# An attention and gated-FFN kernel on one Trainium2 core: two products go from VectorE to GpSimd, and the head gets ten more matmuls

## The chip, the core and the metric

The kernel runs on one core of a Trainium2 chip. Five engines work side by side, each through its own list of instructions in order: TensorE (PE in the profile, its weight loads PEld), VectorE (DVE), ScalarE (ACT), GpSimd (POOL) and SyncE (SP), which here issues nearly all of the transfers. They meet through semaphores. The metric is the device time of one execution in microseconds.

## The reference, cut to what matters

Inputs are float32: x of 1 x 2048 x 512, wqkv 512 x 1536, wo 512 x 512, w1 and w3 512 x 1792, w2 1792 x 512.

```
xn  = layernorm(x)                              # over the 512
q,k,v = split(xn @ wqkv)                        # 32 heads of 16
p   = softmax(q k^T / 4)                        # full, 2048 x 2048 for each head
s   = (p v for all heads, side by side) @ wo
h   = silu(xn @ w1) * (xn @ w3)
g   = silu(h @ w2)
out = x + s * g
```

In the reference the layer-normalised xn feeds both the attention and the gated network.

## The kernel before, in words

**Stages.** A head of some 160 us normalises and transposes x, splits each operand of the projections into a high and a low part (a product is then three matmuls), and computes q, k and v. Then comes the long steady part, up to about 1640 us, and a tail that multiplies by wo and adds x.

**The steady part** is 32 *phases*: 16 pairs of heads times two halves of the queries. Three kinds of products share PE. For the exponentials, L625 makes a 128 x 512 tile of scores in a PSUM bank and ACT turns it into exponentials (L628). For the row maxima of the next phase, L389 makes such a tile and DVE reduces it (L391). For the gated network ("gate"), L855 adds up halves of products in a third kind of bank. All three use only half of PE's rows, so two of them run side by side. Between them, groups of L638 multiply the exponentials by the values into one fixed bank `pv`, whose row 17 of each 32 collects the sums. Seven banks are shared by the three kinds; a bank comes back when ACT or DVE has read it.

**What sets the order.** PE's order is a string of some 8,700 letters, `ORDER_OF_ISSUE`: s and S for scores, m and M for maxima, f and F for gate halves, v for values. While the program is written out, a small model of the engines (`Model`) keeps estimated times; steps of the other engines are put into their lists when the model says that their input is ready. `soon(engine, ready, ...)` books such a step of the gate, and `settle()` writes it out when its time has come. `mod.work(engine, start, cost)` books an engine's estimated time.

**End of a phase.** `take_out` (L641 to L665) is a chain of steps, some microseconds of model time apart: ACT copies `pv` to `ot` (L644); SP spreads the sums over 128 partitions (L650); DVE takes reciprocals (L652); SP writes them out (L654) and reads them back, broadcast, into the one tile `rb` (L657); 16 us of model time later the product `ot * rb` follows (L659, DVE), then POOL rounds it to a high part `oh` (L662) and takes the low part `ol` (L663); SP stores both (L674). The last three phases go another way, so 29 pass here.

**The gate** (`gate`, L706) runs over four blocks of 512 tokens, each in two halves of the 1792. POOL does its products (L725, L726, L741 to L743) and splits the streamed weights w1, w3, w2 (L321, L322; the weights come through L307, four raw tiles in flight, splits up to five units ahead). At the end of each block four row tiles close (`summed`, L756): DVE adds the second half's sum to `part` (L765, `add`), ACT takes a tanh (L771, `bend`), one product makes silu from it (L775, `times`), and SP stores the tile (L776). A silu is written as y * (1 + tanh) with the factors of a half left for later.

**The head.** `busy(n)` (L447) runs n transposes of the identity into `pv`, whose content nobody reads: 12 at the start and 6 more behind the first tile's transposes (L479). Behind them stand the first token tile's value products (L506).

Of the kernel before, what the change touches and what calls it, by code (L numbers as in the profile page):

```python
# [12 lines left out]
ALU = mybir.AluOpType  # L13
# [127 lines left out]
def raw(ap):  # L141
    return ap.bitcast(F32)
# [3 lines left out]
def kernel(ctx: ExitStack, tc: tile.TileContext, x, wqkv, wo, w1, w3, w2, out):  # L146
    nc = tc.nc
# [40 lines left out]
    rb = const.tile([P, 512], F32, name="rb")  # L188
# [20 lines left out]
    def xt_pair(pool):  # L209

        return [pool.tile([P, KC, 512], F32R, tag=f"xt{v}", name=f"xt{v}", bufs=1) for v in "hl"]
# [84 lines left out]
    mod = Model()  # L296
# [120 lines left out]
    with tc.tile_pool(name="pro", bufs=1) as pro, tc.tile_pool(name="pros", bufs=1) as pros:  # L417
# [29 lines left out]
        def busy(n):  # L447
            for _ in range(n):
                nc.tensor.transpose(pv[:, :P], ident, ident)

        busy(12)
        xts = {}

        def spread(t):
# [186 lines left out]
    def take_out(p, half):  # L641

        ot = work.tile([P, 512], F32, tag="ot", name="ot", bufs=2)
        nc.scalar.copy(ot, pv)  # L644
        yield
        sums = work.tile([P, 16], F32, tag="sums", name="sums", bufs=2)
        rec = work.tile([P, 16], F32, tag="rec", name="rec", bufs=2)
        rd = dram.tile([4, 512], F32, name=f"rd{p * 2 + half}")
        for j in range(4):
            nc.sync.dma_start(sums[32 * j:32 * j + 32, :], ot[32 * j + DH:32 * j + VW, :])  # L650
        yield
        nc.vector.reciprocal(rec, sums)  # L652
        yield
        nc.sync.dma_start(rd.rearrange("j (a b) -> (j a) b", b=16), rec)  # L654
        yield
        for j in range(4):
            nc.sync.dma_start(rb[32 * j:32 * j + DH, :], rd[j:j + 1, :].to_broadcast([DH, 512]))  # L657
        yield
        nc.vector.tensor_mul(ot, ot, rb)  # L659
        oh = work.tile([P, 512], F32R, tag="oh", name="oh", bufs=1)  # L660
        ol = work.tile([P, 512], F32R, tag="ol", name="ol", bufs=1)
        nc.gpsimd.tensor_scalar(oh, ot, 1.0, 1.0, op0=ALU.mult, op1=ALU.mult)  # L662
        nc.gpsimd.tensor_sub(ol, ot, raw(oh))  # L663
        yield
        store_rows(p, half, oh, ol)  # L665

    def store_rows(p, half, oh, ol):
        for qb in range(2):
            for h in range(2):
                j, r = 32 * (qb * 2 + h), (p % 4) * 32 + h * DH  # L670
                for s, v in enumerate((oh, ol)):
                    b = half * 2 + qb
                    dst = raw(o_d[p // 4][s][b]) if p < NP - 1 else raw(ov[b][s][p // 4])
                    nc.sync.dma_start(dst[r:r + DH, :], raw(v)[j:j + DH, :])  # L674
# [5 lines left out]
    def soon(engine, ready, bank, what):  # L680

        owed.append((ready, engine, bank, what))
        owed.sort(key=lambda e: e[0])
# [8 lines left out]
    def flush(bank):  # L692

        while any(e[2] <= bank for e in owed):
            e = next(e for e in owed if e[2] <= bank)
            owed.remove(e)
            e[3](e[0])

    def three(lhs, rhs):

        return [(lhs[1], rhs[0]), (lhs[0], rhs[1]), (lhs[0], rhs[0])]
# [4 lines left out]
    def gate():  # L706

        xt = xts[TB - 1]
        number = 0
        for n, b in enumerate(ORDER):  # L710
            part = {}
            for hf in range(HF):
                hs = []
                u = [None]

                def gated(ps, i, u=u):
                    th = ffn.tile([P, 512], F32, tag="th", name="th", bufs=2)
                    nc.scalar.activation(th, ps, AF.Tanh, scale=0.5)
                    mod.work("act", lanes.begins + mod.LATENCY, 0.6)
                    g = u[0] = ffn.tile([P, 512], F32, tag="u", name="g", bufs=2)  # L720
                    nc.scalar.copy(g, ps)
                    free_at[lanes.at_bank[i]] = mod.work("act", 0.0)

                    def times(ready):
                        nc.gpsimd.tensor_scalar(th, th, 1.0, 1.0, op0=ALU.add, op1=ALU.mult)  # L725
                        nc.gpsimd.tensor_mul(g, th, g)  # L726
                        mod.work("pool", ready, 1.9)

                    soon("pool", free_at[lanes.at_bank[i]], i, times)

                def upped(ps, i, f, hs=hs, u=u):
                    if not hs:
                        hs.extend(ffn.tile([P, FH, 512], F32R, tag=f"hs{v}", name="hs", bufs=1) for v in range(2))
                    flush(i - 1)
                    g = u[0]
                    h2 = ffn.tile([P, 512], F32, tag="th", name="h2", bufs=2)
                    nc.scalar.copy(h2, ps)  # L737
                    free_at[lanes.at_bank[i]] = mod.work("act", lanes.begins + mod.LATENCY)

                    def times(ready):  # L740
                        nc.gpsimd.tensor_mul(h2, g, h2)  # L741
                        nc.gpsimd.tensor_scalar(hs[0][:, f, :], h2, 1.0, 1.0, op0=ALU.mult, op1=ALU.mult)
                        nc.gpsimd.tensor_sub(hs[1][:, f, :], h2, raw(hs[0][:, f, :]))  # L743
                        made[i] = mod.work("pool", ready, 3.2)

                    soon("pool", free_at[lanes.at_bank[i]], i, times)

                first = number
                for f in range(FH):
                    for up in range(2):  # L750
                        i, w = wts.next()
                        mms = [m for k in range(KC) for m in three([v[:, k, :] for v in w], [v[:, k, :] for v in xt])]
                        yield lambda j, mms=mms: mms[j], 3 * KC, [i], (lambda ps, i, f=f: upped(ps, i, f)) if up else gated, None
                        number += 1

                def summed(ps, i, t, hf=hf, part=part, b=b):  # L756
                    if hf == 0:
                        part[t] = ffn.tile([P, 512], F32, tag=f"part{t}", name="part", bufs=1)
                        nc.scalar.copy(part[t], ps)
                        free_at[lanes.at_bank[i]] = released[i] = mod.work("act", lanes.begins + mod.LATENCY)  # L760
                        return
                    y = part[t]

                    def add(ready):
                        nc.vector.tensor_add(y, y, ps)  # L765
                        free_at[lanes.at_bank[i]] = released[i] = mod.work("dve", ready, 0.7)
                        soon("act", released[i], i, bend)

                    def bend(ready):
                        th = ffn.tile([P, 512], F32, tag="u", name="th2", bufs=2)  # L770
                        nc.scalar.activation(th, y, AF.Tanh, scale=0.25)  # L771
                        soon("dve", mod.work("act", ready, 0.6), i, lambda ready: times(ready, th))

                    def times(ready, th):
                        nc.vector.scalar_tensor_tensor(y, th, 1.0, y, op0=ALU.add, op1=ALU.mult)  # L775
                        soon("sync", mod.work("dve", ready, 0.7) + 0.3, i, lambda ready: nc.sync.dma_start(  # L776
                            g_d[b][t * P:(t + 1) * P, :], y))

                    soon("dve", lanes.begins + mod.LATENCY, i, add)

                ws = []
                for t in range(4):

                    def down(j, t=t, first=first, hs=hs, ws=ws):
                        f = j // 3
                        flush(first + 2 * f + 1)
                        if f == len(ws):
                            ws.append(wts.next())
                        w = [v.rearrange("p a b -> p (a b)") for v in ws[f][1]]
                        return three([v[:, f, t * P:(t + 1) * P] for v in hs], w)[j % 3]  # L790

                    if t > 1 and hf == 1 and n + 1 < TB:
                        if t == 2:
                            xt = xt_pair(keep)
                        nc.sync.dma_start(raw(xt[t - 2]).rearrange("p k t -> p (k t)"), raw(xt_d[ORDER[n + 1]][t - 2]))
                    yield down, 3 * FH, [i for i, _ in ws] if t == 3 else [], (
                        lambda ps, i, t=t: summed(ps, i, t)), first
                    number += 1
# [299 lines left out]
    ready = {0: 0.5}  # L1098
# [185 lines left out]
    ot, oh, ol = pt_tile(F32), pt_tile(F32R), pt_tile(F32R)  # L1284
# [20 lines left out]
    for t in range(4):  # L1305
        i, ps = take("o")
# [30 lines left out]
```

## Time and profile before

| | |
|---|---|
| median of three runs | 1761.44 us (1761.28 to 1761.94) |
| profiled execution | 1762.41 us |
| its span, first to last instruction | 1760.3 us |
| PE busy | 99% of the span |
| DVE busy | 84% |
| ACT busy | 71% |
| POOL busy | 40% |
| granted TensorE clock, as the profile gives it | 1.000 |

Rows of instruction groups read: line, engine, operation, tiles out<-in, shapes, count, then total busy us and mean ns of one, then the engine's idle time just before them and what ended it. Rows of waits read: who <- for whom, us in total, times, longest. Rows of a timeline begin with the start in us and the duration; in brackets stands the idle time before it. Rows of stretches read: from:to, length, busy us and count of instructions of each engine named, then granted clock, share of the DMA engines, GB/s. PE's ends are modelled, so its busy time covers short holes between matmuls.

### The profile page before, as it was taken

Reading aid. Unit: us, or ns where it says so; the run is one execution under the profiler, and the core shown is the slowest. Engines: PE = TensorE matmul, PEld = TensorE weight load, DVE = VectorE, ACT = ScalarE, POOL = GpSimd, SP = SyncE. Lnnn points to the kernel's source line nnn. Section 1 sums busy time; section 2 is a strip of 40 time slices with the busy share of each in tenths; the row PEclk is TensorE's granted clock in tenths of the full one; section 3 lists DMA queues with packets and bytes.
Section 4 is the critical chain, followed back from the end, with each engine's and each line's share of the span. In section 5 each row is a group of like instructions: output and inputs, shape, how many; then the busy total and the mean of one; then the engine's idle time right before and its main releaser. Section 6 shows DMA issues by size and latency. Waiting matters only on the chain.

```text
span 1760.3 us, 35527 instructions
## 1 busy us (share of the span) xinstructions
PE 1747.2 (99%) x13178; PEld 1028.4 (58%) x13178; DVE 1480.8 (84%) x2452; ACT 1253.5 (71%) x2376; POOL 699.5 (40%) x730
## 2 busy tenths in 40 slices
PE   9999999999999999999999999999999999999998
PEld 7877655555555555555555555565555565556455
DVE  6567998889888998898898898898988897899725
ACT  4223778778768787778778777777777867868871
POOL 3102743346425460545236442555155615551101
PEclk9999999999999999999999999999999999999999
DMA  8656213132323221231433131132322221330542
GB/s 276 243 200 206 59 40 70 47 70 59 74 81 84 59 58 47 61 81 47 92 97 68 51 77 32 50 68 74 100 79 62 74 44 53 100 90 28 186 147 96
DMA packets 146797, 155.36 MB, mean 88 GB/s; under 512 B 42304, under 2 KB 100672, under 8 KB 143648
## 3 DMA queue, kind: packets, MB, share of 16 engines
q1 hardware_dynamic: 145760, 151.52, 31.2%
q8 instruction: 104, 1.70, 0.4%
q10 hardware_dynamic: 864, 1.57, 0.2%
q14 instruction: 69, 0.57, 0.1%
HBM read 107.97 MB, written 44.02 MB: 86 GB/s over the span
## 4 chain that ended last, share of the span: by engine, by line
PE 90%; issue 4%; DVE 3%; DMA 1%; ACT 1%; SPq 1%; POOL 0%; DVEq 0%; ACTq 0%; POOLq 0%
PE pv L638 26%; PE f L855 25%; PE e L625 17%; PE m L389 13%; PE m L506 3%; DVE mp L391 2%; PE e L195 2%; PE e L199 2%; PE e L197 2%; DVE ot L659 1%; ACT pt L628 1%; PE m L479 0%; PE m L403 0%; DMA inh<-in_A_x_dram 0%; SPq L892 0%
## 5 line engine op out<-in xcount | busy, mean ns | idle before, releaser
L391 DVE TENSOR_REDUCE mp<-m 128x1 f32<-128x512 f32 x2048 | 1299.1, 684 | 162.4 <-PE m L389 93.0
L628 ACT ACTIVATE pt<-e 128x512 f32<-128x512 f32 x2048 | 1092.8, 604 | 318.7 <-PE m L389 133.0
L625 PE MATMUL e<-qs,ks 64*128 64x512 f32 x2048 | 717.3, 415 | 2.8 <-DVE mp L391 2.6
L389 PE MATMUL m<-ks,qs 62*128 62x512 f32 x2048 | 694.3, 412 | 1.6 <-DVE mp L391 1.1
L638 PE MATMUL pv<-pt,vt 128*17 128x512 f32 x4096 | 515.0, 597 | 0.0
L625 PEld LDWEIGHTS e<-qs,ks 64*128 64x128 f32 x2048 | 340.0, 184 | 273.0 <-ACT pt L628 92.2
L389 PEld LDWEIGHTS m<-ks,qs 62*128 62x128 f32 x2048 | 336.8, 184 | 129.2 <-ACT pt L628 42.5
L638 PEld LDWEIGHTS pv<-pt,vt 128*17 128x17 f32 x4096 | 81.3, 96 | 201.7 <-issue 193.0
L855 PE MATMUL f<-xth,wl 64*128 64x512 f32 x488 | 171.9, 397 | 0.0
L855 PE MATMUL f<-xtl,wh 64*128 64x512 f32 x488 | 171.7, 392 | 0.0
L855 PE MATMUL f<-xth,wh 64*128 64x512 f32 x488 | 169.4, 393 | 0.0
L741 POOL TENSOR_TENSOR h<-g,h 128x512 f32<-128x512 f32 x56 | 72.0, 1285 | 213.3 <-ACT h L737 213.2
L662 POOL TENSOR_SCALAR oh<-ot 128x512 fp32r<-128x512 f32 x29 | 18.3, 630 | 337.6 <-DVE ot L659 304.8
L855 PE MATMUL f<-wh,hs 64*128 64x512 f32 x496 | 149.8, 396 | 0.0
L855 PE MATMUL f<-xth,xel 64*128 64x512 f32 x408 | 147.9, 396 | 0.0
L855 PE MATMUL f<-xth,xeh 64*128 64x512 f32 x408 | 144.9, 392 | 0.0
L855 PE MATMUL f<-xtl,xeh 64*128 64x512 f32 x408 | 144.3, 392 | 0.0
L322 POOL TENSOR_TENSOR wl<-wr,wh 128x512 fp32r<-128x512 f32 x92 | 118.8, 1291 | 7.7
L855 PE MATMUL f<-xeh,hs 64*128 64x512 f32 x400 | 121.2, 393 | 0.0
L322 POOL TENSOR_TENSOR xel<-wr,xeh 128x512 fp32r<-128x512 f32 x76 | 97.9, 1289 | 6.3
L855 PEld LDWEIGHTS f<-xtl,wh 64*128 64x128 f32 x488 | 85.7, 185 | 6.8
L855 PEld LDWEIGHTS f<-xth,wh 64*128 64x128 f32 x488 | 84.6, 185 | 6.4
(178 smaller groups left out, 1994.0 us busy)
## 6 DMA issues: line engine op xcount, KB each, us to landing
wr<-in_B_w_dram SPq DMA_DIRECT2D x168, 256.0 KB
qs<-qk SPq DMA_DIRECT2D x186, 64.0 KB
ks<-qk SPq DMA_DIRECT2D x90, 128.0 KB
qk<-sh SPq DMA_DIRECT2D x32, 256.0 KB
qk<-sl SPq DMA_DIRECT2D x32, 256.0 KB
v<-vrow SPq DMA_DIRECT2D x16, 272.0 KB
xin<-in_A_x_dram SPq DMA_DIRECT2D x16, 256.0 KB
g<-part SPq DMA_DIRECT2D x16, 256.0 KB
```

Source lines behind the costliest of these rows:

```text
L195: nc.tensor.matmul(ps, lhs[1], rhs[0], start=first, stop=False)
L197: nc.tensor.matmul(ps, lhs[0], rhs[1], start=False, stop=False)
L199: nc.tensor.matmul(ps, lhs[0], rhs[0], start=False, stop=last)
L322: nc.gpsimd.tensor_sub(lo, t, raw(hi))
L389: nc.tensor.matmul(ps, qs[p % 2][64 * h:64 * h + KM, q0:q0 + P], ks[p % 2][64 * h:64 * h + KM, c * 512:(c + 1) * 512], start=True, stop=True)
L391: nc.vector.reduce_max(mp[p, half][:, h, qt, c:c + 1], ps, axis=AX.X)
L506: nc.tensor.matmul(ps, lhs, wsp[k][h == 1][:, 2 * D:], start=n == 0, stop=n == len(three) - 1)
L625: nc.tensor.matmul(ps, ks[p % 2][64 * h:64 * h + KR, k * P:(k + 1) * P], qs[p % 2][64 * h:64 * h + KR, q0:q0 + 512], start=True, stop=True)
L628: nc.scalar.activation(pt, ps, AF.Exp, scale=DH ** -0.5)
L638: nc.tensor.matmul(pv[32 * j:32 * j + VW, :], vt[2 * p // GH][:, key, 2 * p % GH + j % 2, :], pt, start=key < 2 if last else k == 0, stop= ...
L741: nc.gpsimd.tensor_mul(h2, g, h2)
L855: nc.tensor.matmul(ps, left[r], right[r], start=starts and lane == 0, stop=ends and lane == 1)
```

## The change

Three edits. The first `busy` has 22 transposes in place of 12. In `take_out`, the product `ot * rb` is POOL's in place of DVE's. In the gate's `times`, DVE's one instruction (th + 1) * y becomes two of POOL's, one that adds 1 to th in place and one that multiplies; the step is booked on POOL with 1.9 us of model time, where it was booked on DVE with 0.7.

```diff
-        busy(12)
+        busy(22)
...
-        nc.vector.tensor_mul(ot, ot, rb)
+        nc.gpsimd.tensor_mul(ot, ot, rb)
         oh = work.tile([P, 512], F32R, tag="oh", name="oh", bufs=1)
         ol = work.tile([P, 512], F32R, tag="ol", name="ol", bufs=1)
         nc.gpsimd.tensor_scalar(oh, ot, 1.0, 1.0, op0=ALU.mult, op1=ALU.mult)
...
-                        soon("dve", mod.work("act", ready, 0.6), i, lambda ready: times(ready, th))
+                        soon("pool", mod.work("act", ready, 0.6), i, lambda ready: times(ready, th))
 
                     def times(ready, th):
-                        nc.vector.scalar_tensor_tensor(y, th, 1.0, y, op0=ALU.add, op1=ALU.mult)
-                        soon("sync", mod.work("dve", ready, 0.7) + 0.3, i, lambda ready: nc.sync.dma_start(
+                        nc.gpsimd.tensor_scalar(th, th, 1.0, 1.0, op0=ALU.add, op1=ALU.mult)
+                        nc.gpsimd.tensor_mul(y, th, y)
+                        soon("sync", mod.work("pool", ready, 1.9) + 0.3, i, lambda ready: nc.sync.dma_start(
                             g_d[b][t * P:(t + 1) * P, :], y))
```

Behind the head PE's list is the same as before, and so is ACT's. In the changed kernel lines from 777 on have a number higher by one. Three places show what moves.

DVE, where the first gate block closes its last two tiles beside the end of a phase (about 517 us of the profile before). `mp` are the maxima, `part` the gate's tile. Before:

```order
L391 TENSOR_REDUCE mp<-m 128x1 x6
L765 TENSOR_TENSOR part<-part,f 128x512
L391 TENSOR_REDUCE mp<-m 128x1
L775 SCALAR_TENSOR_TENSOR part<-th_7144,part 128x512
L659 TENSOR_TENSOR ot<-ot,rb 128x512
L391 TENSOR_REDUCE mp<-m 128x1 x8
L765 TENSOR_TENSOR part<-part,f 128x512
L391 TENSOR_REDUCE mp<-m 128x1
L775 SCALAR_TENSOR_TENSOR part<-th_7309,part 128x512
```

With the change, the same place:

```order
L407 TENSOR_TENSOR ml<-m,mh 16x128
L391 TENSOR_REDUCE mp<-m 128x1 x6
L765 TENSOR_TENSOR part<-part,f 128x512
L391 TENSOR_REDUCE mp<-m 128x1 x9
L765 TENSOR_TENSOR part<-part,f 128x512
L391 TENSOR_REDUCE mp<-m 128x1 x13
```

The two products between the maxima are gone; the sum L765 stays on DVE.

POOL at the same place (`wh`, `wl`, `xeh`, `xel` are weight splits). Before:

```order
L742 TENSOR_SCALAR hs<-h_6446 128x512
L743 TENSOR_TENSOR hs<-h_6446,hs 128x512
L662 TENSOR_SCALAR oh<-ot 128x512
L663 TENSOR_TENSOR ol<-ot,oh 128x512
L321 TENSOR_SCALAR wh_7291<-wr 128x512
L322 TENSOR_TENSOR wl_7292<-wr,wh_7291 128x512
```

With the change, from the block's third tile on:

```order
L775 TENSOR_SCALAR th_7156<-th_7156 128x512
L776 TENSOR_TENSOR part<-th_7156,part 128x512
L659 TENSOR_TENSOR ot<-ot,rb 128x512
L662 TENSOR_SCALAR oh<-ot 128x512
L663 TENSOR_TENSOR ol<-ot,oh 128x512
L321 TENSOR_SCALAR wh_7304<-wr 128x512
L322 TENSOR_TENSOR wl_7305<-wr,wh_7304 128x512
L321 TENSOR_SCALAR xeh<-wr 128x512
L322 TENSOR_TENSOR xel<-wr,xeh 128x512
```

The block's third product (L775, L776) and the phase's product (L659) now stand ahead of the rounding and the splits; the block's fourth product comes behind four splits.

SP, stores and loads at the end of the first gate block. Before:

```order
L650 DMA sums<-ot 32x1x16 x4
L776 DMA g_126<-part 128x512
L795 DMA xth<-xt_66 128x2048
L654 DMA rd_6546<-rec 128x16
L657 DMA rb<-rd_6546 16x512 x4
L776 DMA g_126<-part 128x512
```

With the change:

```order
L650 DMA sums<-ot 32x1x16 x4
L777 DMA g_126<-part 128x512
L796 DMA xth<-xt_66 128x2048
L654 DMA rd_6556<-rec 128x16
L657 DMA rb<-rd_6556 16x512 x4
L777 DMA g_126<-part 128x512
```

Here the order is the same, with each store of g now waiting for POOL; elsewhere a store of g stands a few transfers later than before.

## The prediction

> **What bounds the kernel now.** I read the page first, then the groups of instructions, then the waits of the weight loads, and last the stretches just behind the instructions that the change removes.
>
> ```profile
> span 1760.3 us, 35527 instructions
> PE 1747.2 (99%) x13178; PEld 1028.4 (58%) x13178; DVE 1480.8 (84%) x2452; ACT 1253.5 (71%) x2376; POOL 699.5 (40%) x730
> L391 DVE TENSOR_REDUCE mp<-m 128x1 f32<-128x512 f32 x2048 | 1299.1, 684 | 162.4 <-PE m L389 93.0 <-PE e L625 43.6 <-PE f L855 13.4
> L659 DVE TENSOR_TENSOR ot<-ot,rb 128x512 f32<-128x512 f32 x29 | 23.0, 792 | 0.0
> L775 DVE SCALAR_TENSOR_TENSOR part<-th,part 128x512 f32<-128x512 f32 x16 | 11.5, 718 | 2.0 <-ACT th L771 1.7
> ```
>
> PE sets the end. It is counted busy 99% of the span, but a matmul's modelled end lies about 0.39 us behind its start while starts follow each other every 0.11 us or so, so a short hole between two starts is not seen as idle. The second engine is DVE with 84%, nearly all of it the row maxima (L391). Each of these frees a PSUM bank that PE needs for a later product. The two lines that the change takes from DVE sum to 23.0 + 11.5 = 34.5 us. That is the most they could be worth if every nanosecond of DVE were a nanosecond of PE.
>
> Is PE held by DVE at all? These are waits of the weight loads between 190 and 1640 us.
>
> ```profile
> PEld e L625 <- DVE mp L391: 82.3, 109, 1.0
> PEld m L389 <- DVE mp L391: 28.1, 47, 1.0
> PEld f L855 <- POOL hs L743: 0.9, 1, 0.9
> ```
>
> So loads do wait for a bank that L391 has yet to free, 110 us in all, though much of this lies under matmuls still streaming. POOL is waited for once. To price the removed instructions I cut 29 stretches of four microseconds: just before each L659, from its start, and the four after those. In each row PE's busy time and its matmuls (x) follow the length. Of each set the sum and one to three rows are shown, and the whole steady part ahead of them.
>
> ```profile
> 190.00:1640.00 1450.00, 1445.60 (x11563) 822.79 (x11561) 1290.55 (x2128) 1124.93 (x2122) 640.37 (x659) 1.00 0.26 66
> ...
> 272.20:276.20 4.00, 4.00 (x36) 1.00 0.59 145
> 1620.60:1624.60 4.00, 4.00 (x38) 1.00 0.03 6
> sum 116.00, PE 115.98; mean PE 4.00
> ...
> 276.20:280.20 4.00, 4.00 (x34) 1.00 0.97 133
> 1152.30:1156.30 4.00, 3.42 (x30) 1.00 0.92 129
> 1624.60:1628.60 4.00, 4.00 (x32) 1.00 0.05 17
> sum 116.00, PE 113.01; mean PE 3.90
> ...
> 280.20:284.20 4.00, 4.00 (x32) 1.00 1.17 213
> sum 116.00, PE 116.00; mean PE 4.00
> ```
>
> The whole steady part shows 1450.00 - 1445.60 = 4.40 us of idle PE, and 2.99 us of it lie in the 116 us that follow an L659, 8% of the time. One of them close up:
>
> ```profile
> 1153.11 0.39 PE L855 MATMUL f<-xth,xeh 64*128 64x512 f32 x1
> 1152.30 1.12 DVE L659 TENSOR_TENSOR ot<-ot,rb 128x512 f32<-128x512 f32 x1
> 1153.35 2.56 DVE L391 TENSOR_REDUCE mp<-m 128x1 f32<-128x512 f32 x4
> 1154.08 0.50 PE L389 MATMUL m<-ks,qs 62*128 62x512 f32 x2 [0.58 <-DVE mp L391]
> ```
>
> L659 holds DVE for 1.12 us, the next maximum comes that much later, and PE starts nothing from 1153.11 to 1154.08. Less one ordinary pitch of 0.11 this is 0.86 us lost, of which 0.58 shows as idle. A visible hole is thus 0.27 us longer than it looks.
>
> **The change part by part. L659 to POOL.** PE's and ACT's lists are the same in both kernels apart from ten matmuls at the head, so what DVE no longer does can be taken straight off PE's holes. Two counts from the rows above. The 29 stretches behind L659 hold 985 matmul starts, those before them 1065, those after them 1056. The latter two make 1060 on average, or 0.109 us a start, so 75 starts or 8.2 us are missing. The other count: 14 of the 29 stretches show idle, 2.99 + 14 x 0.27 = 6.8 us, and holes under 0.27 us do not show. I take 7.4, with the 3.0 that show and the instruction's whole 23.0 as ends. The value lies by the counts, since in half of the stretches PE lost nothing that shows, and there L659 was hidden behind a bank that was free in time.
>
> **L775 to POOL.** The same cut for 16 stretches, before and behind it:
>
> ```profile
> sum 64.00, PE 63.90 PEld 29.59 DVE 55.02 ACT 51.64 POOL 12.40; mean PE 3.99 PEld 1.85 DVE 3.44 ACT 3.23 POOL 0.77
> ...
> sum 64.00, PE 63.66 PEld 27.75 DVE 58.88 ACT 43.12 POOL 13.24; mean PE 3.98 PEld 1.73 DVE 3.68 ACT 2.70 POOL 0.83
> ```
>
> Idle is 0.34 us behind it, 0.24 more than ahead of it; one of the two stretches that show it also holds an L659 and is counted already. With 0.27 for each of the two holes that makes 0.8; holes too short to show are put at half of that again, so I take 1.2, ends 0 and 11.5.
>
> **What POOL pays.** The new instructions have the form of lines that stand there now:
>
> ```profile
> L726 POOL TENSOR_TENSOR g<-th,g 128x512 f32<-128x512 f32 x56 | 71.8, 1282 | 4.7
> L725 POOL TENSOR_SCALAR th<-th 128x512 f32<-128x512 f32 x56 | 34.6, 619 | 122.2 <-ACT th L718 122.2
> POOL oh L662 <- DVE ot L659: 304.8, 24, 46.3
> 1139.89 1.73 SPq L657 DMA_DIRECT2D rb<-rd  x4
> ```
>
> 29 x 1.28 + 16 x (0.62 + 1.28) = 67.5 us more, which takes POOL from 640 to about 708 of the 1450 us. What hides it: at 24 of the 29 places POOL already stood waiting for DVE's L659, 304.8 us in all, so the product fits into the wait it replaces. In the case shown its input rb was issued from 1139.89 to 1141.62, over ten microseconds before DVE got to it, so POOL can start at once. At the five places where POOL came late, the rounding behind it (L662, L663) ends up to 1.28 us later. Behind L659 on POOL stand weight splits and the gate's next products. L775's second wait is on SP: the store of g now leaves about 1.2 us later (1.90 against 0.72), with the weight loads and the normaliser's transfers behind it. Cover gone, each costs its lateness; the one wait of 0.9 us for POOL in the rows above says that the cover is thick. I put 0.5 us on this, ends 0 and the slower rival below.
>
> POOL's extra work can also lengthen DVE's own.
>
> ```profile
> L399 DVE TENSOR_SCALAR nm<-mx x32: 174/176/1258, 153.0 to 1663.8; 128x16 f32<-128x16 f32 x32
> ```
>
> The same small instruction takes 176 ns mostly and up to 1258 (shortest, median, longest). That is a rival, priced below. The Trainium skill's page "GPSIMD Engine Reference" (section Key points) says that POOL shares its SBUF interfaces with VectorE, against VectorE instructions in a two-port mode or with two SBUF inputs. By that rule L399 and L659 are what suffers, and the row of L399 agrees; L391, which reads PSUM, would not, and its mean of 684 shows no such tail.
>
> **The head.** Ten more transposes of 128 columns run ahead of the first token block. The last row is a stretch in which PE's busy time follows its length; its matmuls stand without idle time.
>
> ```profile
> 1.36 2.82 PE L449 MATMUL pv<-ident 128*128 128x128 f32 x12 [1.36 <-POOL minus L444]
> 6.00 1.12 PE L479 MATMUL m<-ident,xn 128*128 128x128 f32 x4 [1.82 <-DVE xn L470]
> 8.04 2.05 PE L506 MATMUL m<-wqh,xeh 128*128 128x512 f32 x4
> 8.33 2.70 POOL L490 TENSOR_TENSOR wql<-wr,wqh 128x512 fp32r<-128x512 f32 x2
> 9.90 1.91 PE L506 MATMUL m<-wqh,xel 128*128 128x512 f32 x4
> 11.60 0.85 PE L479 MATMUL m<-ident,xn 128*128 128x128 f32 x4
> 12.21 1.42 PE L506 MATMUL m<-wql,xeh 128*128 128x512 f32 x5
> 15.09 0.60 PE L479 MATMUL m<-ident,xn 128*128 128x128 f32 x4
> 15.44 1.17 PE L506 MATMUL m<-wqh,xel 128*128 128x512 f32 x4
> ...
> 12.00:30.00 18.00, 18.00 (x88) 14.62 (x87) 12.98 (x30) 8.86 (x20) 2.19 (x4) 1.00 0.79 265
> ```
>
> The same four matmuls take 1.91 us at 9.90 and 1.17 at 15.44, the same four transposes 1.12, 0.85 and 0.60. PE runs at half pace until about 12.1, 6.1 us after it began to work without a pause at 6.00. The twelve transposes end near 4.2 and leave a gap of 1.82 us. At their pitch of 0.218 us, 22 reach to 6.16, so the pause is gone and the transposes at 6.00 are at worst 0.16 us late. Counted from 1.36, the same 6.1 us bring the full pace at about 7.5, before the matmuls at 8.04. Two groups of four then take 0.74 us less each, and the transposes at 11.60 0.25 less: 1.7 us. The last low part of the weights comes from POOL at 8.33 + 2.70 = 11.03, its matmul now starts near 13.0, so more than 2.0 us cannot be had. Behind 12 us PE runs on without a hole and carries the gain through, unless transfers hold it. I take 1.5, ends -0.2 and 2.0.
>
> The Trainium skill's "TensorE: Matmul & The Clock Gate" (What's actually happening) gives one free-running window of about 3.4 us of steady work as what opens the clock. By it the full pace would come between 4.8 and 8.2 us, and this term would shift from run to run by some tenths, an estimate that leaves the sum within half a microsecond.
>
> **The sum.** 7.4 + 1.2 + 1.5 - 0.5 = 9.6 us. The profiled execution took 1762.41 us, 2.1 more than its span, and 0.97 more than the median of the runs, 1761.44. So 1762.4 - 9.6 = 1752.8 profiled, and 1751.8 as a median.
>
> **The rivals.** *Nothing, or nearly.* POOL's share rises from 44% to 49% and hits more of DVE's short instructions. L399's mean of 466 ns (14.9 us over 32) is 0.29 above its median; in proportion that grows by 1 us. Were all 32 to take the longest time, DVE would lose 32 x 0.79 = 25 us. At the share that reached PE for L659 (7.4 of 23.0) that is 8 us, which leaves 1.5 of the gain: 1760. For it speaks that the two meet at all, against it that each phase has one L399 and one L659, seldom side by side. The same time would come if the bank that PE lacks were then held by ACT, which is busy 71%.
>
> *Slower.* The fourth product of a gate block stands on POOL behind four weight splits (about 1.9 us each, 7.6 in all), and the store of g on SP waits for it with the next weight loads behind. If PE then lacks weights at the start of the next block, four block ends cost up to 7.6 us each: 30 us against 9.6, 1782 at worst; it decides from 2.4 us a block on. Against it:
>
> ```profile
> POOL xeh L321 <- DMA wr<-in_B_w_dram: 47.4, 3, 39.9
> ```
>
> POOL waits up to 39.9 us for weights without PE noticing, because splits run some units ahead. A store that waits 5 us longer should vanish in that.
>
> *More than forecast.* The holes behind L659 cost more than counted, or a DVE that runs less behind also closes others: up to the 34.5 us of the two lines; I see no more than 16 of it, 1745.
>
> **How the numbers follow.** Forecast 0.74 (1747 to 1757), nothing or nearly 0.13, slower 0.05, more 0.08. A measurement here tells 0.2%, 3.5 us, from no change. Faster by over that is the forecast, the larger gain and a little of the first rival, 0.85; within it 0.10; slower 0.05. For eight times in ten the range runs from 1746.5, some 5 us below the forecast as the larger L775 and L659 ends allow, to 1757.5, where only 40% of the sum arrives.
>
> **What would show it.** Right: the 29 stretches behind the phases' products lose their holes, idle PE in the steady part falls from 4.4 towards 1.5 us, L662 waits no more for DVE, transposes before 10 us take 0.60, and DVE is busy some 34 us less. Wrong: weight loads wait for POOL or for weights (wr), L399's mean rises well over 0.5 us, or PE's holes stay under another name, an ACT exponential.

## The result, and the profile after

The changed kernel takes 1750.37 us (median of six runs, 1749.66 to 1751.04), the kernel before 1761.17 on the same chip (six runs, 1760.35 to 1761.94): a ratio of 0.9938 with a 95% interval of 0.9926 to 0.9951, or 10.8 us less. Forecast were 9.6 us less and 1751.8.

The page of the changed kernel, its span, its engines and its largest group:

```profile
span 1748.5 us, 35521 instructions
PE 1739.4 (99%) x13188; PEld 1027.3 (59%) x13188; DVE 1452.9 (83%) x2407; ACT 1251.7 (72%) x2376; POOL 765.8 (44%) x791
L391 DVE TENSOR_REDUCE mp<-m 128x1 f32<-128x512 f32 x2048 | 1300.4, 685 | 181.2 <-PE m L389 104.2
```

PE is as full as before by its share, and shorter by 7.8 us of busy time. DVE has the same 1300 us of maxima and now idles longer before them, 181.2 us instead of 162.4. The groups that moved, and one that the first rival spoke of:

```profile
L659 POOL TENSOR_TENSOR ot<-ot,rb 128x512 f32<-128x512 f32 x29 | 37.4, 1289 | 67.5 <-DMA rb<-rd 67.5
L776 POOL TENSOR_TENSOR part<-th,part 128x512 f32<-128x512 f32 x16 | 20.6, 1285 | 1.3
L775 POOL TENSOR_SCALAR th<-th 128x512 f32<-128x512 f32 x16 | 9.9, 621 | 151.1 <-ACT th L771 151.1
L399 DVE TENSOR_SCALAR nm<-mx 128x16 f32<-128x16 f32 x32 | 14.0, 436 | 1.1
```

The 67.9 us of products on POOL replace 34.5 on DVE. POOL now stands waiting for its inputs (`rb`, the tanh) before them, where it stood for DVE before. L399 has not become longer.

The same 1440 us of the steady part, first before, then with the change (columns as in the prediction's stretches: PE, PEld, DVE, ACT, POOL, each with its count):

```profile
190.00:1630.00 1440.00, 1435.60 (x11485) 817.38 (x11487) 1281.84 (x2114) 1115.57 (x2104) 635.04 (x654) 1.00 0.27 66
```

```profile
190.00:1630.00 1440.00, 1438.46 (x11567) 822.19 (x11565) 1263.61 (x2084) 1124.25 (x2125) 705.54 (x720) 1.00 0.27 67
```

Idle PE falls from 4.40 to 1.54 us. The count says more: in the same time PE runs 82 matmuls more, and at 1440 / 11567 = 0.124 us each that is 10.2 us of work, nearly the whole gain. The x of a stretch counts every matmul that runs in it, also the few that began ahead of it; over 1440 us that makes no difference, and this count is used below for every kernel.

The place at which the prediction showed a hole of PE (1153.11 to 1154.08 before), in the timeline of the changed kernel:

```profile
1142.01 6.03 DVE L391 TENSOR_REDUCE mp<-m 128x1 f32<-128x512 f32 x9
1145.82 1.28 POOL L659 TENSOR_TENSOR ot<-ot,rb 128x512 f32<-128x512 f32 x1
1146.09 0.39 PE L625 MATMUL e<-qs,ks 64*128 64x512 f32 x1
1147.19 0.62 POOL L662 TENSOR_SCALAR oh<-ot 128x512 fp32r<-128x512 f32 x1
```

Nine maxima follow each other without a break on DVE while POOL multiplies, and the rounding L662 starts right behind the product. PE does not pause: from 1141 to 1149 us no two starts lie more than 0.52 us apart, where the hole of before had 0.97.

What the weight loads still wait for between 185 and 1630 us of the changed kernel:

```profile
PEld e L625 <- DVE mp L391: 79.4, 101, 0.9
PEld m L389 <- DVE mp L391: 24.1, 38, 0.9
PEld f L856 <- POOL ot L659: 0.9, 1, 0.9
PEld f L856 <- POOL hs L743: 0.8, 1, 0.8
```

Waits for DVE remain, though fewer: before, the same stretch had 82.1 and 28.1 us in the first two rows. POOL is waited for twice, 1.7 us in all, as it was before.

The head with the change:

```profile
1.36 4.83 PE L449 MATMUL pv<-ident 128*128 128x128 f32 x22 [1.36 <-POOL minus L444]
6.03 0.60 PE L479 MATMUL m<-ident,xn 128*128 128x128 f32 x4
8.93 0.50 PE L506 MATMUL m<-wqh,xeh 128*128 128x512 f32 x1 [0.16 <-ACT wqh L489]
9.26 1.09 PE L506 MATMUL m<-wqh,xel 128*128 128x512 f32 x4
13.97 1.17 PE L506 MATMUL m<-wqh,xel 128*128 128x512 f32 x4
```

The pause is gone, the transposes at 6.03 take 0.60 instead of 1.12 us, and the matmuls that started at 15.44 start at 13.97, 1.47 us sooner. At full pace PE soon has to wait for weights that ACT is still casting (8.93).

### The profile page after: what moved, and what is told of

Same layout as the page of the kernel before. It is cut to its first block, busy times and chain, and to the rows that moved or that the text cites. A ratio compares the mean times of both kernels' runs of the same rounds, so it can differ in the third digit from the quotient of the medians.

```text
span 1748.5 us, 35521 instructions
## 1 busy us (share of the span) xinstructions
PE 1739.4 (99%) x13188; PEld 1027.3 (59%) x13188; DVE 1452.9 (83%) x2407; ACT 1251.7 (72%) x2376; POOL 765.8 (44%) x791
## 4 chain that ended last, share of the span: by engine, by line
PE 92%; issue 4%; DVE 2%; DMA 1%; SPq 0%; POOL 0%; ACT 0%; ACTq 0%; POOLq 0%
PE f L856 27%; PE pv L638 26%; PE e L625 17%; PE m L389 14%; PE m L506 3%; PE e L195 2%; PE e L199 2%; PE e L197 2%; DVE mp L391 1%; PE m L479 0%; PE m L403 0%; DMA inh<-in_A_x_dram 0%; DMA wr<-in_A_wqkv_dram 0%; DMA ovl<-o 0%; DVE nm L399 0%
## 5 line engine op out<-in xcount | busy, mean ns | idle before, releaser
L391 DVE TENSOR_REDUCE mp<-m 128x1 f32<-128x512 f32 x2048 | 1300.4, 685 | 181.2 <-PE m L389 104.2
L638 PE MATMUL pv<-pt,vt 128*17 128x512 f32 x4096 | 515.0, 597 | 0.0
L638 PEld LDWEIGHTS pv<-pt,vt 128*17 128x17 f32 x4096 | 81.1, 96 | 202.4 <-issue 194.5
L321 POOL TENSOR_SCALAR wh<-wr 128x512 fp32r<-128x512 f32 x92 | 57.3, 622 | 115.0 <-PE e L625 50.6
L725 POOL TENSOR_SCALAR th<-th 128x512 f32<-128x512 f32 x56 | 34.8, 621 | 131.1 <-ACT th L718 131.1
```

The costliest lines, as they stand in the source:

```text
L321: nc.gpsimd.tensor_scalar(hi, t, 1.0, 1.0, op0=ALU.mult, op1=ALU.mult)
L391: nc.vector.reduce_max(mp[p, half][:, h, qt, c:c + 1], ps, axis=AX.X)
L638: nc.tensor.matmul(pv[32 * j:32 * j + VW, :], vt[2 * p // GH][:, key, 2 * p % GH + j % 2, :], pt, start=key < 2 if last else k == 0, stop= ...
```

## The experiments

Each is named by its label. "Before" is the kernel before, timed on the same chip beside each; its median lies between 1761.04 and 1761.60 us, and the row shows the one beside the changed kernel. "Sooner" is taken from two profiled executions: the start of one and the same product by the values (L638) in the kernel before, less its start in the other. Where lines moved, a name's line number differs by one to three.

| kernel | time, us | against before, us | ratio (95%) | matmuls run, 190 to 1630 |
|---|---|---|---|---|
| before | 1761.17 | | | 11485 |
| after | 1750.37 | -10.8 | 0.9938 (0.9926 to 0.9951) | 11567 |
| e1_head | 1760.95 | -0.15 | 0.9999 (0.999 to 1.0007) | 11485 |
| e2_phase | 1754.17 | -6.9 | 0.9963 (0.9951 to 0.9976) | 11537 |
| e3_gate | 1759.65 | -1.45 | 0.9993 (0.9984 to 1.0001) | 11500 |
| e4_left_out | 1752.69 | -8.4 | 0.9953 (0.994 to 0.9967) | 11551 |
| e5_dve_twice | 1781.02 | +19.7 | 1.0111 (1.0097 to 1.0125) | 11342 |
| e6_pool_thrice | 1755.14 | -6.2 | 0.9962 (0.9949 to 0.9975) | 11529 |
| e11_no_head | 1750.98 | -10.6 | 0.9939 (0.9925 to 0.9953) | 11569 |
| e9_neg_folded | 1748.44 | -12.9 | 0.9927 (0.9914 to 0.9939) | 11598 |
| e10_recip_pool | 1748.42 | -12.9 | 0.9927 (0.9914 to 0.9939) | 11594 |
| e12_neg_layout | 1745.55 | -15.5 | 0.9912 (0.9898 to 0.9925) | 11602 |

Where the time is gained, us sooner against the kernel before, by its own time at the left. The rows below the dots are gains within stretches. The first two of them go by all of PE's matmuls; the sum takes each of the 29 places from the last start ahead of L659 to the first one 4 us behind it:

```
time in before             after  e1     e2     e3     e4     e5      e6     e12
170 (end of the head)      1.49   1.43   1.34   0.77   0.85    0.84   0.69   1.55
863                        5.15   1.28   5.00   0.66   4.35   -7.73   0.14   8.68
1549                      10.59   1.35   8.98   2.06   8.33  -16.45   5.53  15.30
1738                      12.10   1.34   8.05   2.80   9.03  -18.71   6.53  16.87
...
29 places of L659, sum     9.3    0.2    9.4    0.7    9.2   -19.2    9.2    9.2
L659 at 1152, to 1155      0.82   0.03   0.83   0.02   0.82   -0.70   0.83   0.83
467 to 485                -0.09  -0.04   0.00  -0.03  -0.01   -0.02  -4.29  -0.04
behind the L775 at 1612    0.39         -2.02   0.41  -0.42   -0.03  -0.07   0.39
```

### One part at a time

e1_head has only the longer `busy`:

```diff
-        busy(12)
+        busy(22)
```

> The kernel before with the 22 transposes at the head alone. My theory: PE then works without a pause from 1.36 us, reaches full pace before the first projections and keeps 1.5 us to the end, so 1.3 to 1.7 us under the kernel before, with nothing changed behind 15 us. Rival, transfers hold the head: the first products are earlier but the gain is given back before the steady part, under 0.5 us in all.

Measured -0.15 us, no change: the rival's time and not the 1.3 to 1.7 expected. In its profiled execution it is 1.43 us sooner at 170 us and keeps that to the end; but so is e2_phase, which has 12 transposes: 1.34. The gain is there against the one profiled execution of before and not against the medians. The heads of kernels with 12 transposes differ among themselves. Timelines of e2_phase and e3_gate, same transposes, then the products that follow:

```profile
6.04 1.12 PE L479 MATMUL m<-ident,xn 128*128 128x128 f32 x4 [1.86 <-DVE xn L470]
9.60 1.08 PE L506 MATMUL m<-wqh,xel 128*128 128x512 f32 x4
```

```profile
6.03 0.66 PE L479 MATMUL m<-ident,xn 128*128 128x128 f32 x4 [1.85 <-DVE xn L470]
7.36 2.40 PE L506 MATMUL m<-wqh,xeh 128*128 128x512 f32 x4
9.56 1.73 PE L506 MATMUL m<-wqh,xel 128*128 128x512 f32 x4
```

With the same pause of 1.85 us, e2 is slow at 6 us and fast at 9.6, e3 fast at 6 us, slow at 7.4 and still partly at 9.6. The clock records that the traces keep give the moment from which the full clock stays: 12.1 us in before, 9.2 to 11.0 in the five other kernels with 12 transposes, 4.4 to 7.3 in the six with 22. So the longer `busy` does bring the full clock sooner, but the moment differs by some 3 us from one execution to the next, and the prediction read it from one execution, the latest of all. Little of it arrives as time: the products that follow the third group of transposes start at 13.7 to 14.6 us in the six kernels with 22 and at 14.1 to 14.7 in the five others with 12, while PE at full pace has to wait for operands (at 8.93 in the timeline above). The Trainium skill's "TensorE: Matmul & The Clock Gate" (What's actually happening) calls the window of the clock gate free-running, so that the moment varies between runs; that the heads differ agrees with it. The 4.8 to 8.2 us that the prediction had taken from that page, for a head without the pause, lie near the 4.4 to 7.3 of the six kernels with 22.

e2_phase has only the phases' product on POOL:

```diff
-        nc.vector.tensor_mul(ot, ot, rb)
+        nc.gpsimd.tensor_mul(ot, ot, rb)
```

> The kernel before with L659 alone on POOL. My theory: the holes of PE behind the 29 instructions close, 9.3 us (the sum by which PE gets ahead at these places between the two traces), and PE's shift grows only there. Rival, the holes were due to something else at the end of a phase (ACT's copy, the transfers): less than 3 us.

Measured -6.9 us: the larger part of the gain, near the prediction's 7.4 and 2.4 short of the 9.3 expected. At the 29 places themselves the 9.3 are there (9.4 in the table); what is missing is lost elsewhere, as shown below. At the L659 of 1152 us, e2 gains 0.83 and after 0.82, where the prediction had counted 0.86.

e3_gate has only the gate's product on POOL (the edit of `times` and of the `soon` ahead of it, as in the change's diff).

> The kernel before with the gate's last product alone on POOL, 16 x two instructions. My theory: 1.0 to 1.6 us gained, at about four of the 16 places. Rival, the stores of g that wait for POOL hold SP and with it the weight loads: nothing gained or up to 3 us lost, with PE waiting for weights at the start of a gate block.

Measured -1.45 us, as expected. The interval touches no change, but 11 runs lie between 1758.83 and 1760.79 and the trace has the same size: 2.80 - 0.77 = 2.0 us sooner, gained at few places behind L775.

The three parts sum to 0.15 + 6.9 + 1.45 = 8.5, and together they give 10.8. The table shows where the rest comes from. Behind the L775 at 1612 us, e2 *loses* 2.02, where the full change gains 0.39. The timeline of e2_phase there:

```profile
1602.23 1.28 POOL L659 TENSOR_TENSOR ot<-ot,rb 128x512 f32<-128x512 f32 x1 [27.07 <-DMA rb<-rd]
1602.46 1.61 DVE L775 SCALAR_TENSOR_TENSOR part<-th,part 128x512 f32<-128x512 f32 x1
1604.72 0.50 PE L625 MATMUL e<-qs,ks 64*128 64x512 f32 x1 [0.60 <-DVE mp L391]
1608.53 1.29 POOL L906 TENSOR_TENSOR wl<-wr,ks 128x512 fp32r<-128x512 f32 x1
1608.54 1.32 DVE L399 TENSOR_SCALAR nm<-mx 128x16 f32<-128x16 f32 x1
1610.51 0.50 PE L625 MATMUL e<-qs,ks 64*128 64x512 f32 x1 [0.81 <-DVE mp L391]
```

L775, still DVE's here, starts 0.23 us into POOL's new product and takes 1.61 us instead of its usual 0.69. Then L399 starts with a product of POOL's and takes 1.32 instead of 0.17. Behind each, PE waits for a maximum, 0.60 and 0.81 us. With both edits there is no L775 on DVE to meet, POOL runs its products one behind the other, and L399 at this place takes 0.17:

```profile
1600.97 1.29 POOL L776 TENSOR_TENSOR part<-th,part 128x512 f32<-128x512 f32 x1
1602.21 1.28 POOL L659 TENSOR_TENSOR ot<-ot,rb 128x512 f32<-128x512 f32 x1
1605.52 0.17 DVE L399 TENSOR_SCALAR nm<-mx 128x16 f32<-128x16 f32 x1
```

So at this place the pair gains 0.39 us, where the parts make -2.02 + 0.41: 2.0 us more together, most of the 2.3 that the sum of the parts lacks. The edits protect each other at L775; that L399 meets POOL here in e2 is a matter of the moment, and e4 below has such a meeting without the product.

### The phases' product left out, and done twice on DVE

e4_left_out leaves the normalising product L659 out altogether; its output is not normalised. It asks what POOL's product still costs.

```diff
-        nc.vector.tensor_mul(ot, ot, rb)
```

> The kernel before with L659 left out: the phase outputs are not normalised (29 of 32 phases), no engine does that product. It shows what DVE's relief is worth without any cost on POOL. My theory: POOL hides its product wholly, so this is as fast as L659 on POOL, within 0.5 us (9 to 10 us under the kernel before). Rival, POOL's 37 us eat part of the gain through late splits or through VectorE's short instructions: this one is faster than L659 on POOL by 1.5 us or more.

Measured -8.4 us. With the product on POOL (e2) it is -6.9, about the difference that the rival named. But the 1.5 us between them lie at the one place of the meeting: -2.02 for e2, -0.42 for e4 (where L399 meets POOL all the same). At the 29 places the two agree within a tenth of a microsecond each. Here a product on POOL thus costs as little as none, unless it meets a DVE instruction that also works from SBUF.

e5_dve_twice is the kernel before with the product done a second time, on DVE, one right behind the other; its output is scaled twice.

```diff
         nc.vector.tensor_mul(ot, ot, rb)
+        nc.vector.tensor_mul(ot, ot, rb)
```

> The kernel before with DVE doing L659 twice in a row (29 phases are normalised twice; the output is another). It doubles the suspected cost. My theory, a hole of PE opens when DVE's delay outlasts the banks that are free: where one product already makes a hole (19 of 29 places) the second adds its whole 0.68 to 0.79 us, elsewhere part of it, 13 to 23 us more than the kernel before (1774 to 1784). Rival, each product costs its share as in the trace before (7 to 9 us for 29): 1768 to 1770. Rival, DVE has room: under 3 us.

```profile
L660 DVE TENSOR_TENSOR ot<-ot,rb 128x512 f32<-128x512 f32 x29 | 23.0, 792 | 0.0
L661 DVE TENSOR_TENSOR ot<-ot,rb 128x512 f32<-128x512 f32 x29 | 20.4, 702 | 1.0
```

Measured +19.7 us for 20.4 us of DVE, within the 13 to 23 expected. The first product cost 8.4 of its 23.0 (e4), the second nearly its whole time. The places at which the first product did no harm had only so much slack: at the L659 of 1152, where taking it away gained 0.82, doubling it loses 0.70; all 29 places lose, 0.2 to 1.0 us each, where 21 had gained. That DVE holds PE is shown from both sides, and a price read as a share of an instruction's time holds in one direction only.

### The product three times on POOL

e6_pool_thrice is the changed kernel with L659 done three times on POOL; its output is scaled three times. It asks when the slower rival, POOL late with weights or products, comes true.

```diff
         nc.gpsimd.tensor_mul(ot, ot, rb)
+        nc.gpsimd.tensor_mul(ot, ot, rb)
+        nc.gpsimd.tensor_mul(ot, ot, rb)
```

> The changed kernel with POOL doing L659 three times in a row (29 phases are normalised three times over; the output is another): 2 x 29 x 1.29 = 75 us more on POOL. My theory, POOL's waits hide it: 0 to 3 us over the changed kernel, that through VectorE's short instructions that meet a busy POOL. Rival, the cover is thin and the slower case was near: late splits or stores hold PE, 10 us or more.

Measured 1755.14, 4.8 us over the changed kernel for 2 x 37.4 = 75 us more on POOL: more than the 0 to 3 expected, less than the rival's 10. Nearly all of it falls at one place, 4.29 us from 467 to 485 us, behind the L659 at 464. The last of the three products ends there at 466.7; the gate's own product is late in turn:

```profile
472.77 1.26 POOL L745 TENSOR_TENSOR hs<-h,hs 128x512 fp32r<-128x512 f32 x1
```

and PE there:

```profile
469.31 1.91 PE L638 MATMUL pv<-pt,vt 128*17 128x512 f32 x16
471.16 0.50 PE L858 MATMUL f<-wh,hs 64*128 64x512 f32 x1
474.09 0.49 PE L858 MATMUL f<-wh,hs 64*128 64x512 f32 x1 [2.43 <-POOL hs L745]
475.44 1.91 PE L638 MATMUL pv<-pt,vt 128*17 128x512 f32 x8
```

PE starts nothing from 471.16 to 474.09, since its next gate matmul reads an `hs` that POOL finishes late. Behind that, eight products take the 1.91 us that sixteen took ahead of it: the clock is at half. The granted clock of the stretches stands third from the end of each row:

```profile
470.00:474.00 4.00, 1.66 (x14) 0.30 (x6) 0.48 (x1) 0.77 (x2) 3.83 (x4) 1.00 0.51 129
474.90:478.30 3.40, 3.40 (x18) 0.98 (x14) 2.39 (x5) 0.79 (x2) 0.00 (x0) 0.50 0.24 72
```

A clock of 0.50 over 3.4 us is 1.7 us of work lost, on top of the 2.7 lost in the pause (2.93 less an ordinary 0.2); together that is about the 4.29. It begins at 474.90, 0.8 us after PE has started again. The granted clock of the whole is 0.998 in three of the five executions (1755.14 to 1756.33 us) and 0.999 in the two others (1753.68 and 1753.98), so the half-pace stretch is probably not in every one. The slower rival's mechanism thus exists, with one form that it did not have: the wait itself can be followed by slow work. POOL's slack at nearly all other places covers three times the product.

### Without the longer head

e11_no_head is the changed kernel with 12 transposes.

```diff
-        busy(22)
+        busy(12)
```

> The changed kernel with 12 transposes at the head, as before: both products on POOL and nothing else. Three readings of the 10.8 us differ here. The head is worth 0.2 us (as the head alone gave in its median) and the two products together are worth more than one by one (6.9 + 1.45), because with both on POOL no two-input product is left on VectorE beside the ones on POOL: 1750.3 to 1750.8. The head is worth its 1.5 us and got lost only when alone: 1751.6 to 1752. The products simply add up and the head makes up the rest: 1752.4 to 1753.

Measured 1750.98, 10.6 us under its own before (1761.6); the changed kernel is 10.8 under its. In absolute time it lies 0.2 us above the first of the three readings, on a chip whose before is 0.4 higher as well. The ten matmuls are worth 0.2 us, as in e1.

### What else DVE does on SBUF

The meeting in e2 pointed to L399, the sign of the maxima, which the first rival had named. In the changed kernel it still meets POOL, here at 208 us:

```profile
208.54 1.27 POOL L726 TENSOR_TENSOR g<-th,g 128x512 f32<-128x512 f32 x1
208.68 1.16 DVE L399 TENSOR_SCALAR nm<-mx 128x16 f32<-128x16 f32 x1
```

e9_neg_folded takes it away: the maxima are transposed with their own sign, and the two instructions that read the result from PSUM take the sign with them. What is computed stays the same.

```diff
-        nm = keep.tile([P, 16], F32, tag="nm", name="nm", bufs=2)
-        nc.vector.tensor_scalar_mul(nm, m, -1.0)
...
-        nc.tensor.transpose(ps[:16, :P], nm, ident)
+        nc.tensor.transpose(ps[:16, :P], m, ident)
...
-        nc.vector.tensor_copy(mh, ps[:16, :P])
-        nc.vector.tensor_sub(ml, ps[:16, :P], raw(mh))
+        nc.vector.tensor_scalar(mh, ps[:16, :P], -1.0, None, op0=ALU.mult)
+        nc.vector.scalar_tensor_tensor(ml, ps[:16, :P], -1.0, raw(mh), op0=ALU.mult, op1=ALU.subtract)
```

> The changed kernel without L399: the maxima are transposed with their sign and the two instructions behind (L406, L407), which read PSUM, take the minus along. My theory, L399's meeting with POOL (13 of 32 times 419 to 1257 ns against 175) makes most of the 3.4 us of holes that are left at these places: 2.0 to 3.5 us under the changed kernel. Rival, the holes belong to L397 and the transposes beside them: under 1 us, with holes of the same size in the trace.

Measured 1748.44, 1.9 us under the changed kernel, just short of the 2.0 expected. From 190 us on PE starts 31 matmuls more than after (11598 against 11567), or 3.8 us; but it came out of the head some 2.5 us later than after did (at 170 us it is 1.00 behind before, after 1.49 ahead). There the products by the weights are slower: from 30 to 150 us, where 1.7 of the 2.5 us are lost, PE runs 546 matmuls in e9, 551 in after and 552 in e12. One group of them in e9, then in e12 (below; the changed kernel has the same 390):

```profile
L197 PE MATMUL e<-xel,wqh 128*128 128x512 f32 x64 | 25.2, 394 | 0.0
```

```profile
L197 PE MATMUL e<-xel,wqh 128*128 128x512 f32 x64 | 24.9, 390 | 0.0
```

These matmuls do the same as before. What had changed ahead of them was only that the two small tiles `nm` were gone, so that later tiles may lie elsewhere.

e10_recip_pool is e9 with the phases' reciprocals (L652) on POOL, as a power of -1, held in a new small tile `inv`.

```diff
+    inv = const.tile([P, 16], F32, name="inv")
+    nc.gpsimd.memset(inv, -1.0)
...
-        nc.vector.reciprocal(rec, sums)
+        nc.gpsimd.tensor_tensor(rec, sums, inv, op=ALU.pow)
```

> The kernel without L399 and with the reciprocals of the sums (L652, 29 x 0.24 us) on POOL too, as a power of -1. My theory: the 1.4 us of holes in stretches that hold an L652 close, 0.8 to 1.6 us under the kernel without L399. Rival, POOL waits in its list for the sums to land and what stands behind is late, or the gain is lost in new meetings on the shared memory port: no gain, or slower.

```profile
L652 POOL TENSOR_TENSOR rec<-sums,inv 128x16 f32<-128x16 f32 x29 | 84.5, 2912 | 30.4 <-DMA sums<-ot 30.4
```

Measured 1748.42, the same as e9, as the rival had it. A power takes POOL 2.9 us for 16 elements a partition, and the 7.0 us that it takes off DVE (29 x 243 ns) move nothing.

e12_neg_layout is e9 with the room of `nm` kept and unused:

```diff
+        keep.tile([P, 16], F32, tag="nm", name="nm", bufs=2)
```

> The kernel without L399, with the room of its tile nm (two buffers of 64 bytes a partition) kept though nothing uses it. Without the room the matmuls of 512 columns in the head took 394 to 395 ns in place of 390 to 392 and PE lost about 2 us of its lead between 12 and 170 us. My theory, that comes from the places of the later tiles in SBUF, shifted by the room: with it the head is as fast as in the changed kernel and the whole is 1.3 to 2.2 us under the kernel without L399 (1746.3 to 1747.3). Rival, the slower matmuls came from something else (that execution, or the two rewritten instructions): 1748.0 to 1748.9, with 394 to 395 ns again.

Measured 1745.55 (1745.25 to 1745.66), 2.9 us under e9, more than the 1.3 to 2.2 expected, and 4.8 under the changed kernel: the fastest of all. Its head is as soon as that of after (1.55 at 170 us), and the matmuls are back at 390 ns. The place shown above, now:

```profile
208.42 1.28 POOL L725 TENSOR_TENSOR g<-th,g 128x512 f32<-128x512 f32 x1
208.44 0.68 DVE L391 TENSOR_REDUCE mp<-m 128x1 f32<-128x512 f32 x1
```

A maximum runs beside POOL's product at its ordinary 0.68 us. That the room of two tiles of 64 bytes a partition is worth 2 us or more is shown by e9 against e12; which tiles' places make matmuls slower, and why, stays open.

## Why the prediction was right, and where its terms were off

**What bounds it.** "PE sets the end" and DVE holds it: shown from both sides, by e4 (-8.4 us without the product) and e5 (+19.7 with two).

**L659, 7.4 us.** Right in its mechanism, too small in size. In the traces PE gets ahead by 9.3 us at the 29 places in the changed kernel, and by 9.2 to 9.4 in e2 and e4. The one hole shown was read well, 0.86 against the 0.82 gained. But 21 places gain where 14 had shown idle, so the count of visible holes (6.8) missed a third of them. The other count (8.2) took the x of a stretch for starts: 985, 1065 and 1056 are the matmuls that run in the stretches, and those that start there are 864, 958 and 952. By these 91 are missing, and at 116 / 955 = 0.121 us some 11 us: near, too, but no better than an estimate. That e2's 6.9 lies so close to 7.4 is luck: it is the 9.3 less the 2.0 lost at the meetings of POOL with L775 and L399 and a few smaller losses.

**L775, 1.2 us.** 1.45 alone in the medians, 2.0 in that trace, 1.4 in the trace of the changed kernel at the twelve places that hold no L659 within 6 us: right. What the prediction did not see is that it also makes room for the other edit: a two-input product of DVE that would have met POOL's new one.

**The head, 1.5 us.** Wrong in size: 0.15 (e1) and 0.2 (after against e11). The full pace came as early as forecast, at 5.9 us in the changed kernel and by 7.3 in all six with its head. The step that failed is the price, "Two groups of four then take 0.74 us less each, and the transposes at 11.60 0.25 less". It takes the slow pace until 12.1 for a property of the kernel before, and that was the execution's own: the five other kernels with 12 transposes had their full clock for good at 9.2 to 11.0 us. The profiled 1762.41 lay 0.97 over the median of its runs, and the prediction took that difference off for the whole sum without asking whether it belonged to this term.

**What POOL pays, 0.5 us.** No price at the 29 places (e2 and e4 agree there), and DVE's other SBUF work met POOL no more than before: L399 436 ns against 466. In the full change the term is about nothing; in e2 alone it is 1.5.

**The sum.** 9.6 against 10.8. The 10.6 us that the changed kernel gains behind 170 us in its trace are the 9.3 of L659 and the 1.4 of L775, and the head adds some 0.2 by the medians. So L659 was 1.9 us too small, the head 1.3 too large, and POOL's 0.5 was not paid. That the first error covered the second is luck.

**The rivals.** *Nothing, or nearly* fell: L399's mean did not rise. But its mechanism is real, in the changed kernel and before: taking L399 away, its 14.0 us on DVE and its meetings with POOL, gained another 4.8 us (e12); in its trace 4.7 of them lie at places where L399 had met POOL. *Slower* fell: 1.7 us of waits for POOL in the steady part as before, no wait for weights; e6 shows where it begins. *More than forecast* fell as a time, since 1745 is far off; but its reason held in part: the holes behind L659 cost 1.9 us more than counted.

**What would show it.** The holes behind the phases' products are gone, idle PE is 1.54 ("towards 1.5"), L662 waits no more for DVE, the transposes take 0.60. DVE is busy 27.9 us less by the page and not 34: the groups' own times, summed over DVE, fall by 33.8 (1502.5 to 1468.7). Both sums are above the page's 1480.8 and 1452.9, since neighbours overlap in the records and the page counts that time once.

## What to carry to other kernels

When an engine off the critical path frees the buffers of one on it, cut the trace into stretches behind the suspect instruction and count there what the critical engine lost: here that came within 1 to 3 us of the 9.3 really lost, and no single count deserves more trust. It is not the suspect's own time, of which about two fifths reached the end when it was taken away and nearly all when it was doubled. Look next at which instructions on VectorE and GpSimd work from SBUF side by side, since moving one of two can make the other one slow and moving both helped more than their sum; and read a term that hangs on the start of a kernel from several executions, not one.

## What the runs showed of the hardware that was not expected

**Meetings of DVE and POOL.** The lengths of three of DVE's instructions in e2_phase (shortest, median, longest, ns):

```profile
L775 DVE SCALAR_TENSOR_TENSOR part<-th,part x16: 678/692/1606, 482.5 to 1629.9; 128x512 f32<-128x512 f32 x16
L399 DVE TENSOR_SCALAR nm<-mx x32: 174/176/1319, 151.6 to 1655.8; 128x16 f32<-128x16 f32 x32
L391 DVE TENSOR_REDUCE mp<-m x2048: 616/682/694, 63.4 to 1654.8; 128x1 f32<-128x512 f32 x187
```

The two that work on SBUF alone become as long as the product of POOL's beside them and more; the 2048 that read PSUM never exceed 694 ns. DVE's L659 in the kernel before was of the first kind: the six of its 29 that met a product of POOL's took 0.84 to 1.62 us, the 23 others, with POOL idle beside them, 0.68. The Trainium skill's "GPSIMD Engine Reference" (Specifications) states contention with DVE for instructions in a two-port mode or with two SBUF inputs. L775 and L391 agree with it. L399 has one input, so it falls under it only if it runs in such a mode, which no run here shows.

**The clock after a short pause.** In e6 a pause of 2.9 us between two starts was followed by 3.4 us at half the clock. In e3, PE stood still for 1.85 us, from 4.18 to 6.03, with the full clock granted; from 7.5 us on it had half of it for 3.4 us:

```profile
4.20:7.50 3.30, 1.45 (x11) 1.22 (x12) 2.04 (x6) 1.81 (x3) 2.16 (x2) 1.00 0.99 335
7.60:10.90 3.30, 3.30 (x8) 1.97 (x8) 3.13 (x6) 1.24 (x2) 2.82 (x4) 0.50 0.68 232
```

The Trainium skill's "TensorE: Matmul & The Clock Gate" (What's actually happening) has the clock fall after at least one idle window of about 3.4 us; here it fell after pauses of less, twice.

**The recorded clock.** The first 12 us of e3_gate, then of the kernel before:

```profile
0.00:12.00 12.00, 8.77 (x36) 6.66 (x37) 6.23 (x13) 4.57 (x7) 8.66 (x17) 0.86 0.73 238
```

```profile
0.00:12.00 12.00, 8.82 (x32) 7.55 (x33) 6.26 (x13) 4.14 (x6) 8.27 (x17) 1.00 0.72 240
```

The clock is given as 0.86 in the one and as full in the other, though before was at half pace for all of its work in that stretch and ran fewer matmuls (32 against 36). The trace of before holds no clock record ahead of 12.11 us, and the column counts time without a record as full. At the head the durations of like matmuls tell the pace.
